# More staging buffers for the first MLP's weights, and its output matrix converted among the second batch's attention steps

## The chip, the cores and the metric

One core of a Trainium2 chip runs the whole program. The metric is the device time of one execution in microseconds; the median of three runs is quoted.

## What is computed

The reference is an attention block with a memory, followed by two MLPs. Cut to what matters:

```python
scores = scale * q @ k.T                     # B=4, H=8, S=576, D=64, causal
local  = softmax(scores) @ v
mem    = phi(q) @ M_prev / (phi(q) @ z_prev)
x = g * mem + (1 - g) * local                # -> 2304 tokens x 512
x = silu(x @ w_in1) @ w_out1                 # 512 -> 2048 -> 512
y = mish(x @ w_in2) @ w_out2                 # 512 -> 2048 -> 512
```

Everything is float32 outside. Inside, each factor of the MLPs' products is split into two float16 parts (a high and a low one), and three matmuls stand for one product.

## The kernel before

The work of a whole program is first recorded as a list of operations, each with a priority, its possible engines and the regions it reads and writes (`Plan.add`). `Plan.issue` (line 97) then goes through a model of the engines: whenever an engine is free it takes, of the operations that are ready, the one with the lowest priority number. The order in which operations are taken is the order in which the instructions stand on each engine, and on the chip each engine goes through them in that order. A priority or a buffer that is changed thus moves instructions everywhere.

**Attention.** There are 32 visits: 16 pairs of heads, first with query tiles 0 and 1 (`VISITS`, line 28), later with tiles 2 to 4. A step is one query tile of one visit: `stage_a` makes scores, exponentials and a DMA transpose of the probabilities (line 559), `stage_b` multiplies with v and the memory, `stage_c` transposes the result (line 610) and writes it to `xd`. Visits 0 to 3 (eight steps) are batch 0; their output is chunk 0 of 256 tokens. `load_kq` and `load_vm` fetch a visit's inputs.

**Weights.** Each MLP's weights are 16 units of 1 MB (`NU`); units 0 to 7 are w_in, 8 to 15 are w_out. `weight_unit` (line 653) loads a unit into a staging buffer `r` and joins its two 32-bit halves to a float32 matrix `w` in slot u + 2 of the array `w_first`: two ScalarE copies, two or three VectorE operations of 1024 columns, and a ScalarE square whose sum gives the maximum `topw`. When eight units are done, `weight_scale` takes the maximum over them (a reduction `mx<-topw` at line 331, a diagonal and a matmul with ones, then the small operations on `cvec`), and `weight_split` writes the high and low parts, one ScalarE copy and one VectorE operation for each unit, in slot u.

The staging buffers of the first MLP's first half are the two `ws` tiles and two pieces of memory that are free early (`g`, `xh`); the second half has the two `ws` alone. A buffer is free again when the unit's square (line 671) has written over it.

**MLP.** A chunk's x is loaded from `xd`, its maximum taken (`chunk_x`), and copied by ScalarE and VectorE to two parts in `xh`. A chunk has eight steps: `gemm1` (24 matmuls, `banks<-xh,w`), `hidden` (tanh from `xsc` on ScalarE, a VectorE operation on `ga` at line 322, and its split into `g`), `gemm2` (24 matmuls, `banks<-g,w`). The first GEMM of layer 0 has two banks, which `hidden` frees. `xsc` holds products of the chunk's scale and of `cvec`, which w_out's maximum completes, so no `hidden` runs before w_out's `weight_scale`. On TensorE the GEMMs have the lowest priority; attention goes first where it is ready.

**Priorities.** The steps of batch 0 have -1.5e5, w_in's units -2e5 and w_out's -1e5 (`W_PRIO`); the steps of the later batches have 2.3 for each step's number, from 18.4 on.

Of the kernel before, what the change touches and what calls it, by code (L numbers as in the profile page):

```python
# [9 lines left out]
F32 = mybir.dt.float32  # L10
F32R = mybir.dt.float32r
U32 = mybir.dt.uint32
# [26 lines left out]
NU = NF  # L39
SPARE = 2  # L40
# [138 lines left out]
def attn_moe_moe2_kernel(ctx: ExitStack, tc: tile.TileContext, kq, vm, beta, w1, w2, out):  # L179
# [22 lines left out]
    def buf(name, shape, dt, n=1):  # L202
        ts = [sb.tile([128, *shape], dt, name=f"{name}_{i}") for i in range(n)]
        return ts

    def ring(tiles):
        state = [0]

        def take():
            state[0] += 1  # L210
            return tiles[(state[0] - 1) % len(tiles)]

        return take
# [14 lines left out]
    w_first, = buf("w", [(NU + SPARE) * 2048], F16)  # L228
# [5 lines left out]

    ws = buf("ws", [1024, 2], U32, 2)
    early = [t[:, 0:4096].bitcast(U32).rearrange("p (n t) -> p n t", t=2) for t in (g_tile, xh)]
    wstages = [ring(ws + early), ring(ws)]
    ga = buf("ga", [2 * TOK], F32, 2)

    spares = [w_first[:, 2048 * NU + 1024 * i:2048 * NU + 1024 * i + 1024].bitcast(F32) for i in range(2 * SPARE)]  # L240
# [55 lines left out]
    def slot(l, u):  # L296
        return (w_first, w_second)[l][:, 2048 * u:2048 * u + 2048]
# [38 lines left out]
    def act(prio, out, in_, func, scale=1.0, bias=0.0):  # L336
        plan.add(prio, [c_act(out, in_, func, scale, bias)], [out], aps(in_, scale, bias) + [tables])

    def ts(prio, out, in0, s1, op0, s2=None, op1=None):
        plan.add(prio, [c_ts(out, in0, s1, op0, s2, op1)], [out], aps(in0, s1), shared=not ps(in0))  # L340

    def stt(prio, out, in0, s, in1, op0, op1):
        plan.add(prio, [c_stt(out, in0, s, in1, op0, op1)], [out], aps(in0, s, in1), shared=not ps(in0) and not ps(in1))

    def tt(prio, out, in0, in1, op, es=("DVE",)):
        plan.add(prio, [(*c_tt(e, out, in0, in1, op), WAIT_R * i) for i, e in enumerate(es)], [out], aps(in0, in1),
                 shared=not ps(in0) and not ps(in1))
# [34 lines left out]
    def dma(prio, out, in_, writes=None, reads=None):  # L382
        nbytes = 128 * cols(out) * SIZE[out.dtype]
        plan.add(
            prio, [("SP", 475, lambda: nc.sync.dma_start(out=out, in_=in_))],
            [out] if writes is None else writes, [in_] if reads is None else reads, tail=nbytes / 360)
# [49 lines left out]
    def load_kq(v, prio):  # L436
        p, _, nk = VISITS[v]
        n = min(S, 128 * nk)
        t = kqr()
        rk[v], rq[v] = t[:, 0, 0:n], t[:, 1]  # L440
        dma(prio, t[:, :, 0:n], kq[p].rearrange("p (t s) -> p t s", t=2)[:, :, 0:n], reads=[])

    def load_vm(v, prio):
        p, _, nk = VISITS[v]
        n = nk * 2 * (D + 1)
        t, rm[v] = rvr()[:, 0:n], rmr()
        rv[v] = t.rearrange("p (n e d) -> p n e d", n=nk, e=2)
        dma(prio, t, vm[p, :, 130:130 + n], reads=[])
        dma(prio, rm[v], vm[p, :, 0:130], reads=[])
# [43 lines left out]
    def prep_phi(v, i0, i1, prio):  # L493

        if v not in er:
            er[v] = er_()
        e, src = er[v][:, 64 * i0:64 * i1], rq[v][:, 64 * i0:64 * i1]
        act(prio, e, src, AF.Exp)
        act(prio, src, src, AF.Relu)
        stt(prio, e, e, 1.0, src, ALU.min, ALU.add)  # L500
# [65 lines left out]
    def stage_b(n, prio):  # L566

        v, qt = STEPS[n]
        R = min(128, S - 128 * qt)
        nk = qt + 1  # L570
        v1, v2, gvv = vv[v]
        vb = bank[6 + qt % 2]
        if qt < 4:
            pw = pts.pop(n).rearrange("p (s e k) q -> p s k e q", s=2, e=2)
        else:
            pw = pts.pop(n).rearrange("p (s k) (e q) -> p s k e q", s=2, e=2)
        ms = []
        for e in range(2):
            o = vb[0:R, 65 * e:65 * e + 65]
            for kb in range(nk):  # L580
                hi, lo = pw[:, 0, kb, e, :], pw[:, 1, kb, e, :]
                ms += [
                    (o, hi, v1[:, kb, e, :], kb == 0, False),
                    (o[:, 0:D], hi, v2[:, kb, e, :], False, False),
                    (o, lo, v1[:, kb, e, :], False, kb == nk - 1)]
        mm(prio, ms + [(vb[0:R, 130:260], er[v][:, 128 * qt:128 * qt + R], rm[v], True, True)])
        if not last(n):
            return
        m = 1 + qt % 2
        g = banks[0:R, 512 * 6:512 * 8].rearrange("p (b c) -> p b c", b=2)[:, 0:m, 0:260].rearrange("p b (a c) -> p b a c", a=4)  # L590
        den, t4, x = denr()[0:R, 0:m], t4r()[0:R, 0:m], xr()[0:R, 0:m]
        each = lambda y: y[0:R].unsqueeze(1).to_broadcast([R, m, 4])
        tt(prio, den, g[:, :, :, D], each(eps), ALU.add)
        other(prio, "DVE", 165, lambda: nc.vector.reciprocal(out=den, in_=den), [den], [den])
        tt(prio, den, den, each(gvv), ALU.mult)
        tt(prio, t4, g[:, :, :, 0:D], den.unsqueeze(3).to_broadcast([R, m, 4, D]), ALU.mult)
        tt(prio, x, t4[:, :, 0:2], t4[:, :, 2:4], ALU.add, ("POOL", "DVE"))
        xts[n] = (x, R)

    def stage_c(n, prio):  # L600

        if not last(n):
            return
        v, qt = STEPS[n]
        p = VISITS[v][0]
        x, R = xts.pop(n)
        m = 1 + qt % 2
        for i in range(m):
            x2, o = x[:, i].rearrange("p e d -> p (e d)"), bank[6 + i][:, 260:260 + R]
            plan.add(prio, [("PE", 56, lambda o=o, x2=x2: nc.tensor.transpose(o, x2, ident[0:R, 0:R]))], [o], [x2, ident],  # L610
                     edge=(107, 56))
        xo = xor_()[:, 0:m * R]
        copy(prio, xo.rearrange("p (b c) -> p b c", b=m),
             banks[:, 512 * 6:512 * 8].rearrange("p (b c) -> p b c", b=2)[:, 0:m, 260:260 + R])
        b, hp = divmod(p, H // 2)
        t0, n = column(b, 256 * (qt // 2)), m * R
        dma(prio, xd[128 * hp:128 * hp + 128, t0:t0 + n], xo, writes=[("xd", hp, hp + 1, t0, t0 + n)])
# [35 lines left out]
    def weight_unit(l, u, prio):  # L653

        r, w = wstages[int(l > 0 or u >= NU // 2)](), slot(l, u + SPARE).bitcast(F32)  # L660
        t = w.bitcast(U32)
        dma(prio, r, W[l][u].bitcast(U32).rearrange("p (n t) -> p n t", t=2), reads=[])
        low, high = r[:, :, 0], r[:, :, 1]
        act(prio, w, high.bitcast(F32), AF.Abs, 2.0**-112)
        ts(prio, t, t, 3, ALU.logical_shift_left)
        stt(prio, t, high, 0x80000000, t, ALU.bitwise_and, ALU.bitwise_or)
        act(prio, low, low, AF.Copy, 2.0**-29)
        tt(prio, t, t, low, ALU.add, ("DVE", "POOL"))
        top = topw[l][:, u:u + 1]

        plan.add(prio, [("ACT", 0.833 * 1024 + 200, lambda: nc.scalar.activation(  # L671
            out=low.bitcast(F32), in_=w, func=AF.Square, accum_out=top))], [top, low], [w, tables])
# [90 lines left out]
    D_B, D_C, D_Q, D_K, D_P, D_V, D_S = 2.5, 3.2, 4.0, 4.0, 3.0, 6.0, 0.5  # L763
    A_RATE, MOE_B, L_V = 2.3, -1e6, 0.0
    att_prio = lambda n, d=0: A_RATE * (n + d) + (ATT_B if n < N0 else 0)
    MOE, W_PRIO, ATT_B = MOE_B, (-2e5, -1e5), -1.5e5

    def prep(v, prio):
        if VISITS[v][1][-1] >= 2:
# [5 lines left out]
    def attention(n0, n1, sbs):  # L775

        for n in range(n0, n1):
            if 0 <= n - LAG - 1 < NS:
                stage_c(n - LAG - 1, att_prio(n - LAG - 1, D_C))
            if 0 <= n - LAG < NS:  # L780
                stage_b(n - LAG, att_prio(n - LAG, D_B))
            if n < NS:
                pr_ = att_prio(n)
                v, qt = STEPS[n]
                qts = VISITS[v][1]
                if qt == qts[0] and v + 1 < len(VISITS):
                    load_kq(v + 1, pr_)
                stage_a(n, sbs, pr_)
                if qt == qts[0]:
                    prep_v(v, att_prio(n, D_B) - D_V)  # L790
                    if v + 1 < len(VISITS):
                        load_vm(v + 1, att_prio(n, L_V))
                if qt == 0 and 2 in qts:
                    prep_q(v, 1, att_prio(n + 2) - D_Q)
                if qt == qts[0]:
                    prep_phi(v, 2 * qts[0], min(2 * qts[-1] + 2, S // 64), att_prio(n, D_B) - D_P)
                if qt == qts[-1] and v + 1 < len(VISITS):
                    prep(v + 1, att_prio(n + 1) - D_K)
# [119 lines left out]
```

## Time and profile before

| | us |
|---|---|
| median of three runs | 1025.33 (1025.13 to 1026.48) |
| the profiled execution's own time | 1025.4 |
| its span | 1023.6 |
| TensorE matmul busy in the span | 948.2 (93%) |
| VectorE busy | 673.4 (66%) |
| ScalarE busy | 642.5 (63%) |
| GpSimd busy | 273.9 (27%) |

The profile has a row for each instruction with its start, its duration, its engine, its line in the code, and what it writes and reads. PE is TensorE's matmul, DVE is VectorE, ACT ScalarE, POOL GpSimd; SPq is the queue of SyncE, which issues nearly all DMAs. A time in brackets is how long the engine stood idle ahead of a row, with what released it. PEclk is the mean granted clock of TensorE as a share of full speed. Consecutive instructions of one engine overlap a little in the rows.

### The profile page before, as it was taken

To read this page: it belongs to the slowest core of one execution; us is meant where nothing else is said; L and a number is where in the kernel's file an instruction comes from. 1 tells how busy PE (TensorE), PEld (TensorE's weight loads), DVE (VectorE), ACT (ScalarE), POOL (GpSimd) and SP (SyncE) were. 2 spreads that over 40 slices of the span, in tenths; PEclk is the share of its full clock that TensorE was granted. 3 is DMA by queue.
4 is the path that set the end of the run, shared out by engine and by line. 5 is a ranking of instruction groups with operands and counts; after the bars stand their busy time and mean duration, and the time that the engine had idled before them with its cause. 6 is when DMAs were issued, how large, how long until landed. Compare 5 with 4: busy or idle time off the path is not lost.

```text
span 1023.6 us, 20794 instructions
## 1 busy us (share of the span) xinstructions
PE 948.2 (93%) x8364; PEld 732.2 (72%) x8364; DVE 673.4 (66%) x1231; ACT 642.5 (63%) x1095; POOL 273.9 (27%) x280
## 2 busy tenths in 40 slices
PE   2436589999999999999999999999999999999998
PEld 1225478888888888888888888766676766766665
DVE  6988687787787878777757756754544545544433
ACT  7977665666666756756667676744555545555544
POOL 1110123343343433432322522212212122222221
PEclk9956589999999999999999999999999999999999
DMA  9767924775787767845353341100100101000000
GB/s 322 230 148 208 228 58 114 162 187 133 183 156 150 151 137 148 176 114 130 105 199 104 104 146 61 42 30 14 42 22 21 32 12 42 22 21 22 1 21 21
DMA packets 149904, 107.93 MB, mean 105 GB/s; under 512 B 111152, under 2 KB 139312, under 8 KB 145712
## 3 DMA queue, kind: packets, MB, share of 16 engines
q1 hardware_dynamic: 149664, 106.60, 40.1%
q8 instruction: 65, 1.06, 0.4%
q14 instruction: 31, 0.25, 0.1%
q10 hardware_dynamic: 144, 0.00, 0.0%
HBM read 66.21 MB, written 14.16 MB: 79 GB/s over the span
## 4 chain that ended last, share of the span: by engine, by line
PE 85%; DMA 6%; DVE 4%; ACT 4%; issue 1%; SPq 0%; POOL 0%; DVEq 0%; POOLq 0%; ACTq 0%
PE banks L375 84%; DMA arena<-arena 2%; DVE w L322 1%; PE banks L610 1%; DMA g<-w 1%; ACT w L314 1%; DMA xs<-xd 1%; ACT arena L314 1%; DMA ws<-w 1%; DVE arena L322 1%; DMA arena<-kq 1%; ACT ws L671 0%; DVE w L328 0%; DVE arena L328 0%; DMA arena<-vm 0%
## 5 line engine op out<-in xcount | busy, mean ns | idle before, releaser
L375 PEld LDWEIGHTS <-w 128*128 128x128 f16 x3456 | 334.8, 98 | 43.3 <-issue 4.2
L375 PEld LDWEIGHTS <-arena 128*128 128x128 f16 (+1 forms) x3168 | 225.5, 101 | 80.1 <-DMA arena<-arena 27.5
L328 POOL TENSOR_TENSOR g<-ga,g 128x512 f16<-128x512 f32 x108 | 144.1, 1335 | 345.7 <-ACT g L314 327.4
L375 PE MATMUL banks<-xh,w 128*128 128x256 f16 x1728 | 213.8, 275 | 2.6 <-DVE ga L322 2.6
L375 PE MATMUL banks<-g,w 128*128 128x256 f16 x1728 | 209.8, 273 | 0.1
L375 PE MATMUL banks<-xh,arena 128*128 128x256 f16 x1728 | 198.6, 273 | 0.0
L375 PE MATMUL banks<-arena,g 128*128 128x512 f16 x864 | 197.4, 379 | 0.0
L375 PE MATMUL banks<-arena 128*128 128x65 f16 (+6 forms) x1728 | 119.0, 235 | 62.1 <-DMA arena<-arena 24.1
L375 PEld LDWEIGHTS <-g 128*128 128x128 f16 x864 | 84.5, 98 | 87.6
L314 ACT ACTIVATE ga<-ga 128x512 f32<-128x512 f32 x108 | 67.6, 628 | 77.5 <-DVE ga L319 53.6
L314 ACT ACTIVATE arena<-arena 128x256 f32<-128x256 f32 (+6 forms) x180 | 101.5, 592 | 18.5 <-PE banks L375 9.5
L322 DVE SCALAR_TENSOR_TENSOR ga<-ga,banks 128x512 f32<-128x512 f32 x108 | 73.7, 683 | 54.2 <-ACT ga L314 53.7
L322 DVE SCALAR_TENSOR_TENSOR arena<-arena 128x256 f16<-128x256 f32 (+6 forms) x144 | 106.1, 746 | 3.9 <-ACT arena L314 3.4
L314 ACT ACTIVATE w<-w 128x512 f32<-128x512 f32 x108 | 66.6, 625 | 47.3 <-DVE w L319 26.3
L314 ACT ACTIVATE arena<-banks,arena 128x128 f32<-128x128 f32 (+4 forms) x144 | 73.9, 545 | 33.9 <-DVE arena L546 25.9
L314 ACT ACTIVATE g<-ga 128x512 f16<-128x512 f32 x106 | 66.3, 626 | 28.7 <-DVE ga L322 28.2
L328 POOL TENSOR_TENSOR arena<-arena 128x256 f32<-128x256 f32 (+1 forms) x48 | 44.0, 916 | 139.1 <-DVE arena L328 89.3
L314 ACT ACTIVATE ga<-banks,xsc 128x512 f32<-128x512 f32 x72 | 49.2, 685 | 49.2 <-PE banks L375 45.5
L546 DVE TENSOR_REDUCE arena<-banks 128x2 f32<-128x256 f32 (+3 forms) x80 | 64.3, 804 | 23.8 <-PE banks L375 19.9
L328 POOL TENSOR_TENSOR g<-w,g 128x512 f16<-128x512 f32 x36 | 41.6, 1156 | 126.2 <-ACT g L314 126.2
L375 PEld LDWEIGHTS banks<-arena 128*128 128x128 f32 (+2 forms) x288 | 42.4, 228 | 32.9 <-ACT arena L314 29.6
L319 DVE TENSOR_SCALAR ga<-banks,xsc 128x512 f32<-128x512 f32 x36 | 27.0, 750 | 51.7 <-PE banks L375 51.6
(95 smaller groups left out, 942.0 us busy)
## 6 DMA issues: line engine op xcount, KB each, us to landing
ws<-w SPq DMA_DIRECT2D x28, 1024.0 KB, 5.3
arena<-kq SPq DMA_DIRECT2D x16, 576.0 KB, 5.0
arena<-vm SPq DMA_DIRECT2D x16, 325.0 KB, 3.4
xs<-xd SPq DMA_DIRECT2D x9, 512.0 KB, 4.6
yd<-w SPq DMA_DIRECT2D x36, 128.0 KB, 1.9
xs<-yd SPq DMA_DIRECT2D x9, 512.0 KB, 3.8
arena<-kq SPq DMA_DIRECT2D x16, 256.0 KB, 3.4
xd<-arena SPq DMA_DIRECT2D x32, 128.0 KB, 2.5
```

What stands on the lines that cost most here:

```text
L314: return ("ACT", ns, lambda: nc.scalar.activation(out=out, in_=in_, func=func, scale=scale, bias=bias))
L319: return ("DVE", ns, lambda: nc.vector.tensor_scalar(out=out, in0=in0, scalar1=s1, scalar2=s2, op0=op0, **kw))
L322: return ("DVE", 1.04 * cols(out) + 160, lambda: nc.vector.scalar_tensor_tensor(out=out, in0=in0, scalar=s, in1=in1, op0=op0, op1=op1))
L328: return (e, ns, lambda: eng.tensor_tensor(out=out, in0=in0, in1=in1, op=op))
L375: nc.tensor.matmul(out=o, lhsT=l, rhs=r, start=a, stop=z)
L546: other(prio, "DVE", 1.04 * cols(both) + 146, lambda: nc.vector.tensor_reduce(out=m1, in_=both, axis=AX, op=ALU.max, negate=True), [m1], [ ...
L610: plan.add(prio, [("PE", 56, lambda o=o, x2=x2: nc.tensor.transpose(o, x2, ident[0:R, 0:R]))], [o], [x2, ident], edge=(107, 56))
```

## The change

The eight units of w_in get eight staging buffers: to `ws`, `g` and `xh` come four pieces of `w_first` itself, slots 10 to 17, which the first half doesn't fill. The eight units of w_out get five: the two `ws`, slots 14 and 15, 16 and 17, and 8 and 9; the last of these and the two `ws` serve again for units 13 to 15. `w_out`'s priority goes from -1e5 to 15, so that its units 8 to 15 stand at 23 to 30, in the range of the second batch's attention steps (18.4 for step 8 to 34.5 for step 15). The loads `load_kq` and `load_vm` get a priority lower by a million, which puts them ahead of the weights' loads.

```diff
-    wstages = [ring(ws + early), ring(ws)]
+
+    room = [w_first[:, 2048 * i:2048 * i + 4096].bitcast(U32).rearrange("p (n t) -> p n t", t=2) for i in range(8, NU + SPARE, 2)]
+    wstages = [ring(ws + early + room[1:] + ws + [room[3], room[4], room[0]] + ws + [room[0]]), ring(ws)]
...
-        r, w = wstages[int(l > 0 or u >= NU // 2)](), slot(l, u + SPARE).bitcast(F32)
+        r, w = wstages[l](), slot(l, u + SPARE).bitcast(F32)
...
-    MOE, W_PRIO, ATT_B = MOE_B, (-2e5, -1e5), -1.5e5
+    MOE, W_PRIO, ATT_B = MOE_B, (-2e5, 15.), -1.5e5
...
-                    load_kq(v + 1, pr_)
+                    load_kq(v + 1, pr_ - 1e6)
...
-                        load_vm(v + 1, att_prio(n, L_V))
+                        load_vm(v + 1, att_prio(n, L_V) - 1e6)
```

The lines behind the first of these stand two further down than in the kernel before: line 559 there is 561 here.

What that makes of the order shows at three places. On SyncE's queue, at the program's start, before (`ws`, `g`, `xh` and `w` as targets are staging buffers, `w` as a source is the weights in HBM; `arena` holds attention's tiles):

```order
L385 DMA arena_98<-vm 128x130
L385 DMA ws_77<-w 128x2048
L385 DMA ws_78<-w 128x2048
L385 DMA g_76<-w 128x2048
L385 DMA xh_75<-w 128x2048
L385 DMA arena_98<-kq 128x2x256
L385 DMA arena_98<-vm 128x260
L385 DMA arena_98<-vm 128x130 x2
L385 DMA arena_98<-kq 128x2x256
L385 DMA arena_98<-vm 128x260
L559 DMA_TRANSPOSE arena_98<-arena_98 128x4x128
```

and after:

```order
L387 DMA arena_98<-vm 128x130
L387 DMA ws_77<-w 128x2048
L387 DMA ws_78<-w 128x2048
L387 DMA g_76<-w 128x2048
L387 DMA xh_75<-w 128x2048
L387 DMA w_73<-w 128x2048 x2
L387 DMA arena_98<-kq 128x2x256
L387 DMA w_73<-w 128x2048 x2
L561 DMA_TRANSPOSE arena_98<-arena_98 128x4x128
```

Eight matrices instead of four stand ahead of the first transpose of attention.

On VectorE, where `xsc` is completed and the first two `hidden` operations follow, before:

```order
L319 TENSOR_SCALAR wsc_0_92<-wsc_0_92 128x1
L328 TENSOR_TENSOR cvec_0_94<-cvec_0_94 128x1
L322 SCALAR_TENSOR_TENSOR arena_98<-arena_98 128x256
L328 TENSOR_TENSOR xsc_89<-cvec_0_94,xsc_89 128x2
L319 TENSOR_SCALAR arena_98<-banks 128x2
L319 TENSOR_SCALAR arena_98<-arena_98 128x2
L546 TENSOR_REDUCE arena_98<-banks 128x2
L322 SCALAR_TENSOR_TENSOR w_73<-w_73,wsc_0_92 128x1024
L322 SCALAR_TENSOR_TENSOR ga_79<-ga_79,banks 128x512
L322 SCALAR_TENSOR_TENSOR ga_80<-ga_80,banks 128x512
```

and after:

```order
L330 TENSOR_TENSOR xsc_89<-cvec_0_94,xsc_89 128x2
L324 SCALAR_TENSOR_TENSOR arena_98<-arena_98 128x256
L330 TENSOR_TENSOR arena_98<-banks,eps_71 128x8
L321 TENSOR_SCALAR arena_98<-banks 128x2
L596 RECIPROCAL arena_98<-arena_98 128x8
L321 TENSOR_SCALAR arena_98<-arena_98 128x2
L330 TENSOR_TENSOR arena_98<-arena_98 128x8
L324 SCALAR_TENSOR_TENSOR ga_79<-ga_79,banks 128x512
L324 SCALAR_TENSOR_TENSOR ga_80<-ga_80,banks 128x512
L321 TENSOR_SCALAR w_73<-w_73,wsc_0_92 128x1024
```

The first split of w_out (`w<-w,wsc`) has moved from ahead of the two `ga` operations to behind them.

On ScalarE, around the copy of chunk 0's x (`xh<-xs,xsc`), after, where `topw<-w` is a unit's square:

```order
L316 ACTIVATE w_73<-w_73 128x1024
L316 ACTIVATE arena_98<-banks,arena_98 128x128
L316 ACTIVATE xh_75<-xs_74,xsc_89 128x1024
L316 ACTIVATE arena_98<-banks,arena_98 128x128
L673 ACTIVATE w_73,topw_0_87<-w_73 128x1024
```

The square there is unit 12's, behind which its buffer (slots 8 and 9, so `w_73` is written) is free for unit 15's load. Before, unit 15 was loaded into a `ws` tile.

## Rows read from the trace of the kernel before

**Rows 1.** Stretches: length, busy us (count) of PE, PEld, DVE, ACT, POOL; PEclk.

```profile
0.00:60.00 60.00, 21.69 (x130) 14.02 (x131) 51.07 (x99) 53.75 (x90) 5.96 (x28) 0.90 0.76 248
60.00:83.64 23.64, 10.85 (x69) 7.01 (x68) 18.62 (x38) 15.62 (x31) 3.78 (x4) 0.50 0.72 172
83.64:118.31 34.67, 22.97 (x147) 16.60 (x147) 29.54 (x65) 25.68 (x50) 3.24 (x6) 0.60 0.83 230
118.31:131.59 13.28, 6.50 (x39) 4.33 (x40) 7.29 (x29) 7.25 (x14) 1.29 (x3) 0.50 0.72 190
131.59:1023.60 892.01, 886.19 (x7979) 690.26 (x7978) 566.89 (x1004) 540.24 (x915) 259.62 (x239) 1.00 0.35 88
```

**Rows 2.** TensorE's waits from 135 us on: total us, times, longest us.

```profile
PE banks L375 <- ACT arena L314: 0.8, 2, 0.6
```

**Rows 3.** Timeline of TensorE: start, us, line, operation, out<-in, count, idle before.

```profile
19.70 1.10 PE L375 MATMUL banks<-arena 128*128 128x65 f16 x8 [12.54 <-DMA arena<-arena]
...
93.38 5.74 PE L375 MATMUL banks<-xh,w 128*128 128x256 f16 x42
...
131.59 6.07 PE L375 MATMUL banks<-xh,w 128*128 128x256 f16 x33 [2.65 <-DVE ga L322]
```

**Rows 4.** Timeline of VectorE, from w_out's maximum to the first `hidden`.

```profile
118.31 0.15 DVE L331 TENSOR_REDUCE mx<-topw 128x1 f32<-128x8 f32 x1
122.61 0.16 DVE L319 TENSOR_SCALAR arena<-banks 128x2 f32<-128x2 f32 x1 [4.15 <-PE banks L375]
...
130.86 1.28 DVE L322 SCALAR_TENSOR_TENSOR ga<-ga,banks 128x512 f32<-128x512 f32 x2
```

**Rows 5.** ScalarE's waits between 60 and 131.6 us.

```profile
ACT w L314 <- DMA ws<-w: 4.6, 4, 2.7
```

**Rows 6.** Issues on SyncE's queue.

```profile
14.11 3.75 SPq L559 DMA_TRANSPOSE arena<-arena  x2
...
102.48 0.34 SPq L385 DMA_DIRECT2D ws<-w  x1
```

**Rows 7.** Timeline of ScalarE: first readings of staged units, and chunk 0's x.

```profile
14.07 1.22 ACT L314 ACTIVATE w<-g 128x1024 f32<-128x1024 f32 x1
...
17.35 1.12 ACT L314 ACTIVATE w<-xh 128x1024 f32<-128x1024 f32 x1
...
89.09 1.14 ACT L314 ACTIVATE xh<-xs,xsc 128x1024 f16<-128x1024 f32 x1
...
109.98 1.14 ACT L314 ACTIVATE w<-ws 128x1024 f32<-128x1024 f32 x1 [0.25 <-DMA ws<-w]
```

**Rows 8.** Groups of VectorE's instructions up to 140 us, each form apart: busy, mean ns.

```profile
L322 DVE SCALAR_TENSOR_TENSOR w<-w,wsc 128x1024 f16<-128x1024 f32 x13 | 17.3, 1357 | 0.0
L322 DVE SCALAR_TENSOR_TENSOR arena<-arena 128x256 f16<-128x256 f32 x19 | 8.5, 455 | 0.0
L328 DVE TENSOR_TENSOR arena<-banks,arena 128x512 f32<-128x512 f32 x8 | 5.5, 689 | 0.1
```

**Rows 9.** Timeline of TensorE behind the gate, at full clock.

```profile
154.21 0.70 PE L375 MATMUL banks<-arena 64*128 64x256 f32 x4
...
154.97 1.47 PE L375 MATMUL banks<-g,w 128*128 128x256 f16 x12
156.28 0.65 PE L375 MATMUL banks<-arena 128*128 128x65 f16 x8
156.77 1.15 PE L375 MATMUL banks<-g,w 128*128 128x256 f16 x9
157.75 0.27 PE L610 MATMUL banks<-ident,arena 128*128 128x128 f32 x1
157.86 0.49 PE L375 MATMUL banks<-g,w 128*128 128x256 f16 x3
```

**Rows 10.** The second maximum of the second MLP's weights: its diagonal on VectorE and TensorE.

```profile
625.47 0.29 DVE L328 TENSOR_TENSOR diag<-ident,mx 128x128 f32<-128x128 f32 x1
...
627.28 0.39 PE L375 MATMUL banks<-diag,onesf 128*128 128x128 f32 x2
```

## The prediction

> **What bounds the kernel now.** I read the stretches first. From 131.59 us to the end TensorE is busy for 886.19 of 892.01 us at a granted clock of 1.00 (2.4 GHz), and the waits of TensorE in that part come to 0.8 us for their largest cause [rows 1, 2]. So behind 131.59 the time is TensorE's own work, and nothing that another engine does there sets the end as long as it stays ahead. In front of it TensorE stands idle for about half of the time, at a clock of 0.50 to 0.60 (that is mostly 1.2 GHz) [rows 1]. The time of the kernel is therefore: the moment at which TensorE's unbroken stretch begins, plus the work that is then still to do. The timeline of TensorE shows that moment: two steps of the first GEMM of chunk 0 run from 93.38 on (42 of their 48 matmuls in one go), then their two banks are full, and the third step starts at 131.59 behind a wait for VectorE's `ga` (line 322), the second operation of `hidden` [rows 3].
>
> What holds `hidden`? The tanh takes its scale from `xsc`, `xsc` takes `cvec`, and `cvec` is finished only by `weight_scale` for w_out, the second half of w1. That begins with the `mx<-topw` reduction at 118.31, when all eight w_out units have been converted [rows 4]. The gate is the conversion of w_out, and the two engines that convert, VectorE and ScalarE, are not full while it waits: VectorE is idle 23.64 - 18.62 = 5.0 us in the stretch to the x of chunk 0, 5.1 in the next and 6.0 in the last, 16.1 us of 71.6 [rows 1]. ScalarE waits 4.6 us for loads of weights in that time [rows 5], and 4.15 us of VectorE's idle time stand right behind the reduction, where it waits for a matmul of attention that is itself queued on TensorE behind a late transpose [rows 4].
>
> **Part by part.** *What is ahead of the gate on VectorE.* In the new order w_out no longer goes ahead of all of the second batch; but four of its eight loads now stand ahead of the first result of attention in SP's order, where it was two, so its conversion can take any free place. Counted in the built order up to the first `ga` operation, VectorE has 228 instructions before and 202 after: all the 16 units' conversions are there in both, and what falls behind the gate is attention of the second batch. The 26: five of 256 wide at 0.46, four of 512 wide at 0.69, one split at 1.36 [rows 8], four score reductions, which are no wider than 512 and which I take at 0.69 too, and twelve small ones (net) at about 0.16, as the small reduction of rows 4. That is 2.3 + 2.8 + 1.4 + 2.8 + 1.9 = 11.2 us of listed time; neighbours on VectorE overlap by up to 0.1 (two of 0.69 take 1.28 in rows 4), and for the 26 I take off 2.2 us: **9.0 us** of real time. If VectorE's idle time stays what it is, the gate moves from 131.6 to **122.6**. If all its idle time behind 60 us went as well, it would be 131.6 - 9.0 - 16.1 = **106.5**. These are my two ends.
>
> *Where between them.* The last w_out unit now decides. Its load goes into the buffer that unit 12 used, so it is issued only when ScalarE has squared unit 12, and in the order that square stands two places behind the copy of chunk 0's x. The copy is at 89.09 [rows 7]; with its 1.14, a small one and a square of about the same length as the copy that is 92. A load took 7.5 us there (issued at 102.48, read at 109.98), and from that reading to the reduction it took 8.3 (109.98 to 118.31) [rows 4, 6, 7]: 107.8. From the reduction to the third step it is 13.3 now; without the 4.15 of the late transpose 9.1. That makes 116.9 without it, and 121.1 with it. I take **117**, since the transpose in question belongs to steps of the second batch of which fewer now stand ahead, and in the new order `hidden` comes ahead of the first split on VectorE.
>
> *What it costs.* The attention that falls behind has to be done by TensorE later, in time that counts. Counted in TensorE's order up to that third step: 18 score matmuls of 128 wide instead of 20, 16 of 256 instead of 20, 126 of 64 and 65 wide instead of 150, 14 memory matmuls instead of 17, 12 transposes instead of 16. In sets: one pair of narrow and two pairs of wide scores, two short and one long product with v, four transposes. At full clock a wide set took 0.76 (154.21 to 154.97), a short product 0.49, a transpose 0.11 [rows 9]; the narrow set I take at no more than the wide one, the long product at 14/8 of the short. Sum: 3 x 0.76 + 2 x 0.49 + 0.86 + 0.44 = **4.6 us**. What VectorE, ScalarE and GpSimd have to do for it is hidden: they are busy for 567, 540 and 260 of the 892 us behind the gate [rows 1]. If that cover were gone, the first to show it would be TensorE's in-order waits for attention.
>
> *Loads moved.* The first transpose of attention now stands behind all eight w_in matrices instead of four. Rows: it was issued at 14.11, and TensorE waited for it until 19.70; the fourth matrix, issued ahead of it, was first read at 17.35 [rows 3, 6, 7]. A matrix takes about 3.3 us (17.35 behind 14.07 [rows 7]), so four more are 13 us. I put this at nothing in the sum, because VectorE and ScalarE have conversions to do in that time and are the fuller engines there, but it is the slower one of the rivals. The Trainium skill (DMA: Bandwidth & Descriptors, section Queues, rings and completion order) says that each DMA engine takes descriptors in ring order, all of SP's from one ring; by that rule the transpose can't overtake the matrices, and the rows above agree; if the delay passes on in full, that is the slower rival below, and if not, the sum stays. The kq and vm loads, given a higher priority, are as many as before, and their buffers still hold them until the older visit is done; I cost them at nothing.
>
> **Sum.** The profiled run took 1025.4 (its span is 1023.6), the median is 1025.33, so I count from the median: 1025.33 - (131.6 - 117) + 4.6 = **1015.3 us**. With the ends: 1025.33 - 25.1 + 4.6 = 1004.8, and 1025.33 - 9.0 + 4.6 = 1020.9.
>
> **Rivals.** *A new gate at the second MLP.* w2's conversion must be done when its first GEMM begins. VectorE had the diagonal of w2's second maximum ready at 625.47 + 0.29, and TensorE took it at 627.28 [rows 10]: 1.5 us of slack. In the new order that matmul stands 156 matmuls ahead of the end of the first MLP instead of 133, 2.5 us earlier in TensorE's stream, and the stream is 10 us earlier; attention, whose memory w2 needs, ends 57 matmuls (6.2 us at 0.109) later in that stream, so some 4 us earlier on the clock. If w2 can't follow any further than that, TensorE waits 10 + 2.5 - 4 - 1.5 = 7 us: 1022; if it can't move at all, 11 us, and the gain is gone: 1026. For it: two buffers pace w2 as before. Against it: VectorE and ScalarE have idle time there too.
>
> *The conversions lose nothing of their idle time, or all of it:* 1020.9 and 1004.8, the ends above.
>
> *Slower: the transposes behind the weights.* If the 13 us of rows 6 and 7 pass on to the whole of batch 0's attention, the x of chunk 0 is copied at 102 instead of 89, the last unit's load is issued 13 us later too, and the gate is at 130: 1025.33 - 1.6 + 4.6 = **1028.3**. It decides from a delay of 10 us on, where the gate's gain equals the 4.6. Against it: in the first 60 us both engines are nearly full (51.07 and 53.75 of 60 [rows 1]), so a delay of 13 at 20 us need not be one at 80. A mild form of the same: the order puts w_out behind steps of the second batch, the gate stays at 131.6 and only the 4.6 us remain: 1029.9.
>
> **Chances.** The forecast (1008 to 1020): 0.62. Nearly no idle time left (1004 to 1008): 0.10. The second gate (1018 to 1026): 0.15. The slower one, with its mild form (1027 to 1031): 0.13. The range 1007 to 1024 holds the forecast's, a part of the next and most of the second gate's. About 0.2% (2 us) is what a measurement of this kernel can tell from no change: faster than 1023.3 is 0.62 + 0.10 + 0.10 of the second gate's; its other 0.05 is within 0.2%, and the 0.13 of the last are slower.
>
> **What would show it.** `mx<-topw` for w_out on VectorE at 106 to 109 instead of 118.31; the third step's matmuls on TensorE at 115 to 119; the copy of chunk 0's x on ScalarE at 88 to 92, as now; the last w_out load issued at about 92; the stretch behind the gate some 4.6 us longer than 892.0, with waits of TensorE of 2 us at most. Wrong: an x of chunk 0 behind 93 (the slower rival); a wait of TensorE for `diag` between 600 and 625 (the second gate); a gate near 122 with VectorE idle as often as now (the sum of work alone).

## The result, and the profile after

The changed kernel took **1012.20 us** (median of four runs, 1011.39 to 1014.18) against 1025.88 for the kernel before in the same comparison: a ratio of 0.987, 95% interval 0.9853 to 0.9887. The forecast was 1015.3, the range 1007 to 1024. The profiled execution took 1011.85; its span is 1009.8.

The stretches of the changed kernel, cut at the same events as [rows 1] (x of chunk 0 loaded, w_out's maximum, the third step); columns as there, the last two being the busy share of the DMA engines and the GB/s they moved:

```profile
0.00:60.00 60.00, 19.76 (x131) 13.55 (x132) 49.83 (x98) 52.88 (x87) 6.40 (x28) 0.91 0.90 275
60.00:85.54 25.54, 11.84 (x73) 7.77 (x72) 20.43 (x41) 18.37 (x37) 3.11 (x4) 0.50 0.74 204
85.54:108.25 22.71, 14.65 (x88) 10.19 (x89) 21.08 (x40) 18.72 (x30) 1.84 (x2) 0.65 0.61 179
108.25:116.28 8.03, 5.99 (x39) 4.22 (x39) 5.72 (x25) 4.74 (x12) 1.15 (x3) 0.50 0.73 214
116.28:1009.80 893.52, 888.86 (x8033) 693.50 (x8032) 561.55 (x1028) 551.97 (x938) 245.62 (x240) 1.00 0.36 90
```

The third step, "the gate" from here on, moved from 131.59 to 116.28, that is 15.3 us; the stretch behind it grew from 892.01 to 893.52, that is 1.5. 15.3 - 1.5 = 13.8 is what the span lost (1023.6 to 1009.8). Most of the gate's gain lies between chunk 0's x and w_out's maximum: 34.67 us before, 22.71 now, with VectorE busy for 21.08 of them. From the maximum to the gate another 5.3 us went (13.28 to 8.03), and ahead of chunk 0's x 1.9 were lost (83.64 to 85.54).

The rows that answer to [rows 3, 4, 6, 7], from the timelines of TensorE, VectorE, ScalarE and SyncE's queue:

```profile
31.97 1.13 PE L377 MATMUL banks<-arena 128*128 128x65 f16 x8
...
116.28 6.24 PE L377 MATMUL banks<-xh,w 128*128 128x256 f16 x33 [0.75 <-DVE ga L324]
```

```profile
85.54 1.22 DVE L333 TENSOR_REDUCE mx<-xs 128x1 f32<-128x1024 f32 x1 [0.30 <-DMA xs<-xd]
...
108.25 0.16 DVE L333 TENSOR_REDUCE mx<-topw 128x1 f32<-128x8 f32 x1 [0.33 <-ACT w L673]
...
115.54 1.28 DVE L324 SCALAR_TENSOR_TENSOR ga<-ga,banks 128x512 f32<-128x512 f32 x2 [0.28 <-ACT ga L316]
```

```profile
92.97 1.13 ACT L316 ACTIVATE xh<-xs,xsc 128x1024 f16<-128x1024 f32 x1
...
100.62 1.17 ACT L316 ACTIVATE w<-w 128x1024 f32<-128x1024 f32 x1 [0.27 <-DMA w<-w]
```

```profile
14.74 1.32 SPq L561 DMA_TRANSPOSE arena<-arena  x1
...
95.50 0.34 SPq L387 DMA_DIRECT2D w<-w  x1
```

TensorE's waits from 116.2 on (total, times, longest): the second is the gate itself, the first one wait at 584.

```profile
PE banks L377 <- POOL g L330: 0.9, 1, 0.9
PE banks L377 <- DVE ga L324: 0.7, 1, 0.7
```

And w2's second maximum on VectorE and its diagonal on TensorE, which answer to [rows 10]; the matmul stands there without an idle time ahead of it:

```profile
609.65 0.16 DVE L333 TENSOR_REDUCE mx<-topw 128x1 f32<-128x8 f32 x1 [0.43 <-ACT ws L673]
```

```profile
611.48 0.39 PE L377 MATMUL banks<-diag,onesf 128*128 128x128 f32 x2
```

### The profile page after: what moved, and what is told of

It is laid out like the page before. It is cut to its first block, busy times and chain, and to the rows that moved or that the text cites. A ratio compares the mean times of both kernels' runs of the same rounds, so it can differ in the third digit from the quotient of the medians.

```text
span 1009.8 us, 20796 instructions
## 1 busy us (share of the span) xinstructions
PE 941.1 (93%) x8364; PEld 729.2 (72%) x8364; DVE 658.6 (65%) x1229; ACT 646.7 (64%) x1100; POOL 258.1 (26%) x277
## 4 chain that ended last, share of the span: by engine, by line
PE 89%; ACT 4%; DMA 3%; DVE 2%; issue 1%; SPq 0%; POOL 0%; ACTq 0%; DVEq 0%; POOLq 0%
PE banks L377 88%; ACT w L316 2%; PE banks L612 1%; DMA ws<-w 1%; DVE w L324 1%; ACT w L673 1%; DMA arena<-arena 1%; DMA xs<-xd 1%; DMA w<-w 1%; ACT arena L316 0%; ACT ws L673 0%; SPq L387 0%; DVE w L330 0%; ACT ws L316 0%; DVE arena L324 0%
## 5 line engine op out<-in xcount | busy, mean ns | idle before, releaser
L330 POOL TENSOR_TENSOR g<-ga,g 128x512 f16<-128x512 f32 x108 | 137.2, 1272 | 352.4 <-ACT g L316 342.0
L377 PE MATMUL banks<-arena 128*128 128x64 f16 (+7 forms) x1728 | 114.4, 232 | 44.3 <-ACT arena L316 29.2
L316 ACT ACTIVATE w<-w 128x512 f32<-128x512 f32 (+2 forms) x124 | 84.8, 693 | 54.9 <-DVE w L321 33.1
L316 ACT ACTIVATE arena<-arena 128x256 f32<-128x256 f32 (+6 forms) x182 | 103.7, 592 | 23.5 <-PE banks L377 14.4
L330 POOL TENSOR_TENSOR arena<-arena 128x256 f32<-128x256 f32 (+1 forms) x47 | 41.2, 876 | 132.0 <-DVE arena L330 96.7
L377 PEld LDWEIGHTS banks<-arena 64*128 64x128 f32 (+2 forms) x288 | 39.9, 222 | 41.0 <-ACT arena L316 36.9
```

The costliest lines, as they stand in the source:

```text
L316: return ("ACT", ns, lambda: nc.scalar.activation(out=out, in_=in_, func=func, scale=scale, bias=bias))
L330: return (e, ns, lambda: eng.tensor_tensor(out=out, in0=in0, in1=in1, op=op))
L377: nc.tensor.matmul(out=o, lhsT=l, rhs=r, start=a, stop=z)
```

## The experiments

Twelve kernels, each beside the kernel before on the same chip (its medians there: 1025.05, 1026.25 and 1025.50 for the three sets). "Gate" is the start of TensorE's third step, "stretch" the rest of the span from there; both are of the profiled execution. Medians of different sets are compared as they stand, though the kernel before itself lies up to 1.2 us apart between the sets.

| kernel | median us | ratio, 95% interval | gate | stretch |
|---|---|---|---|---|
| changed kernel | 1012.20 | 0.987, 0.9853 to 0.9887 | 116.3 | 893.5 |
| buffers alone | 1018.11 | 0.9932, 0.9905 to 0.9959 | 110.9 | 905.9 |
| priority alone | 1024.25 | 0.9992, 0.9979 to 1.0006 | 138.2 | 883.4 |
| loads alone | 1022.98 | 0.9984, 0.9969 to 0.9998 | 127.1 | 895.1 |
| without the loads | 1018.98 | 0.9943, 0.9920 to 0.9965 | 122.7 | 895.0 |
| without the priority | 1016.20 | 0.9904, 0.9883 to 0.9924 | 109.0 | 904.3 |
| w_in in four buffers | 1016.37 | 0.9911, 0.9889 to 0.9932 | 122.7 | 891.9 |
| unit 15 in g | 1010.92 | 0.9853, 0.9834 to 0.9872 | 116.2 | 892.8 |
| early tanh | 1019.79 | 0.9939, 0.9916 to 0.9961 | 103.9 | 914.3 |
| early tanh, w2 in more buffers | 1012.35 | 0.9874, 0.9854 to 0.9894 | 104.6 | 907.3 |
| unit 15 in g, w2 in more buffers | 1010.71 | 0.9861, 0.9840 to 0.9882 | 116.4 | 893.0 |
| unit 15 in g, priority 8 | 1015.58 | 0.9905, 0.9885 to 0.9926 | 107.5 | 908.2 |
| unit 15 in g, priority 22 | 1022.82 | 0.9978, 0.9967 to 0.9989 | 131.7 | 889.4 |

**The three parts apart.** *Buffers alone* takes back the other two (the diff is against the changed kernel):

```diff
-    MOE, W_PRIO, ATT_B = MOE_B, (-2e5, 15.), -1.5e5
+    MOE, W_PRIO, ATT_B = MOE_B, (-2e5, -1e5), -1.5e5
...
-                    load_kq(v + 1, pr_ - 1e6)
+                    load_kq(v + 1, pr_)
...
-                        load_vm(v + 1, att_prio(n, L_V) - 1e6)
+                        load_vm(v + 1, att_prio(n, L_V))
```

> Buffers alone (the staging rings of the changed kernel, the priorities of the kernel before). In the built order VectorE has 175 rows ahead of the first ga operation, where the changed kernel has 197 and the kernel before 223. Theory 'conversion sets the gate, buffers let it run': about 0.35 us for each of 22 rows puts the gate at 108 to 110 (116.3 in the changed kernel), and the attention that falls behind costs TensorE about 3 us: 1007 to 1010. Rival 'the new priority is what pays': near the kernel before, 1022 to 1026. Rival 'the attention loads, which keep their place behind the weights, come late': gate near 109, but waits of TensorE for attention behind it of 3 us and more: 1012 to 1018.

The gate came to 110.9, near the first theory, but the stretch is 12.4 us longer than the changed kernel's, not 3: 1018.11. The third theory's size is missed by 0.1 (1012 to 1018); its reason is looked at below.

```profile
110.90 5.43 PE L377 MATMUL banks<-xh,w 128*128 128x256 f16 x33 [2.80 <-DVE ga L324]
```

*Priority alone* is the new `W_PRIO` on the kernel before:

> w_out's new priority alone, on the kernel before. VectorE has 246 rows ahead of the first ga operation, 23 more than the kernel before. Theory 'conversion sets the gate, buffers let it run': the gate moves some 8 us back, to 138 to 141, TensorE does some 3.5 us of attention ahead of it: 1028 to 1032. Rival 'the new priority is what pays': 1012 to 1018.

Neither came. The gate went back to 138.2, as the first theory said, but the stretch became 8.6 us shorter, not 3.5, and the time is that of the kernel before:

```profile
138.18:1021.60 883.42, 879.21 (x7920) 686.44 (x7919) 560.18 (x970) 541.50 (x910) 252.29 (x238) 1.00 0.34 87
```

TensorE has 59 matmuls fewer behind the gate than in [rows 1] and is busy for 7.0 us less. Counted from each matmul's start to the next one's, the missing attention is 4.6 of the 8.6 us by which the stretch is shorter, about 0.08 for each matmul. Among the rest are 1.2 us of waits for attention that the kernel before has and this one hasn't, and a clock that rose sooner: in the first 10 us behind the gate the granted clock is 0.87 here and 0.76 before (this kernel second).

```profile
131.59:141.59 10.00, 10.00 (x80) 8.04 (x80) 9.79 (x14) 8.55 (x13) 5.07 (x3) 0.76 0.23 58
138.18:148.18 10.00, 10.00 (x80) 7.99 (x80) 9.79 (x15) 9.21 (x16) 5.15 (x3) 0.87 0.04 10
```

Attention that is done while TensorE has nothing else thus pays for a part of a later gate.

*Loads alone* is the earlier kq and vm loads on the kernel before:

> The earlier kq and vm loads alone, on the kernel before. VectorE has 212 rows ahead of the first ga operation, 11 fewer than the kernel before. Theory 'these loads cost and give nothing by themselves': 1022 to 1026, the gate between 127 and 132. Rival 'they take away the short waits of TensorE in attention behind the gate (about 1.4 us of the difference)': those waits gone, and 1 to 2 us less than the first theory's gate alone gives.

1022.98 and a gate of 127.1: the first theory. The short waits for attention did not go (one of 0.96 stands at 197). *Without the loads* is the changed kernel with their old priority:

> The changed kernel with the kq and vm loads at their old priority. VectorE has 206 rows ahead of the first ga operation, 9 more than the changed kernel. Theory 'the loads' priority gives nothing by itself': gate 116 to 120, 1011 to 1016. Rival 'it takes away the short waits behind the gate': 1.5 us and more above the changed kernel even where the gate is the same, with waits of 0.3 to 0.7 us for attention on TensorE.

Both theories fall: the loads' priority is worth 1018.98 - 1012.20 = 6.8 us here, and most of it is in the gate (122.7 against 116.3). SyncE's queue of this kernel shows what changes place: the first two transposes stand behind the loads of the next visits, which stand behind the weights.

```profile
4.50 2.95 SPq L387 DMA_DIRECT2D w<-w  x4
9.39 0.57 SPq L387 DMA_DIRECT2D arena<-kq  x1
11.84 2.79 SPq L387 DMA_DIRECT2D arena<-vm  x2
16.87 0.55 SPq L387 DMA_DIRECT2D arena<-kq  x1
19.27 2.86 SPq L387 DMA_DIRECT2D arena<-vm  x2
24.29 4.01 SPq L561 DMA_TRANSPOSE arena<-arena  x2
```

24.29 instead of 14.74, and TensorE has done 100 matmuls by 60 us instead of 131. Which engine's wait then makes the 6 us was not taken apart further.

**The load of the last unit.** Unit 15 staged in `g`:

```diff
-    wstages = [ring(ws + early + room[1:] + ws + [room[3], room[4], room[0]] + ws + [room[0]]), ring(ws)]
+    wstages = [ring(ws + early + room[1:] + ws + [room[3], room[4], room[0]] + ws + early[:1]), ring(ws)]
```

> The changed kernel with unit 15 staged in g, which is free, and not behind unit 12's square in slots 8 and 9: its load can be issued some 20 us earlier. Theory 'the load chain of the last unit sets the gate' (the prediction's): w_out's maximum 3 to 6 us earlier (102 to 105 where it was 108.25), gate 110 to 113, 1007 to 1010. Rival 'the work of VectorE and ScalarE sets it' (VectorE busy for 21.1 of the 22.7 us ahead of the maximum): maximum within 1.5 us of 108.25, 1010.5 to 1013.5.

The load was issued at 33.27 instead of 95.50, and the maximum did not move:

```profile
33.27 0.38 SPq L387 DMA_DIRECT2D g<-w  x1
```

```profile
108.49 0.16 DVE L333 TENSOR_REDUCE mx<-topw 128x1 f32<-128x8 f32 x1 [0.32 <-ACT g L673]
```

So the load chain did not set the maximum; the work in front of it on VectorE and ScalarE did. Its time is not to be told from the changed kernel's (the intervals overlap).

**Eight buffers for w_in.** w_in staged in the old four, w_out in its five:

> The changed kernel, but w_in staged in the old four buffers (w_out keeps its five). Six instead of eight matrices stand ahead of the first transpose; VectorE has 216 rows ahead of the first ga operation, the changed kernel 197. Theory 'w_in's extra buffers let the conversions run while attention starts': w_in's maximum 4 us later or more, gate 120 to 124, 1015 to 1020. Rival 'eight matrices ahead of the first transpose cost as much as the buffers give': gate 114 to 118, 1009 to 1013.

w_in's maximum came at 51.81 instead of 42.25 and the gate at 122.7: the first theory. Six matrices instead of eight stand ahead of the first transpose there, TensorE's first product is at 25.41 and chunk 0's x at 81.91 instead of 85.54, so the matrices ahead do delay the attention, but the buffers give more than that costs. The later gate isn't the whole account of the 4.2 us, since TensorE has done more attention by then (48 matmuls fewer are left): it also waits ahead of three of the `diag` matmuls that follow (1.2 at 189, 0.5 at 233, 0.8 at 373), where the changed kernel doesn't.

```profile
PE banks L377 <- DVE diag L330: 2.0, 2, 1.2
PE banks L377 <- DVE arena L330: 0.5, 1, 0.5
```

**w_out's priority.** The changed kernel with it back at -1e5:

> The changed kernel with w_out's priority back at -1e5 (buffers and early loads stay). VectorE has 178 rows ahead of the first ga operation, the changed kernel 197. Theory 'the next gate is chunk 1's x, and the new priority is what spares it': the first gate at 108 to 112, but TensorE reaches the end of chunk 0's steps before chunk 1's x is there and waits for its diag by 2 us and more between 150 and 175, with more attention behind the gate: 1013 to 1018. Rival 'with the early loads the new priority is not needed': no such wait, 1006 to 1011.

The gate is 7.3 us earlier and the time 4.0 us longer. The stretch of this kernel:

```profile
108.99:1013.30 904.31, 894.83 (x8076) 697.02 (x8075) 575.61 (x1048) 551.97 (x947) 250.10 (x244) 1.00 0.37 90
```

Against the changed kernel TensorE has 43 more matmuls in it, is busy for 6.0 us more and idle for 4.8 us more (904.31 - 894.83 = 9.48 against 4.66). TensorE's timeline shows where some 2.9 of the idle time stand:

```profile
155.88 0.95 PE L377 MATMUL banks<-arena 64*128 64x256 f32 x4 [0.99 <-ACT arena L316]
...
158.00 0.80 PE L377 MATMUL banks<-diag,onesf 128*128 128x128 f32 x2 [0.95 <-DVE diag L330]
159.19 0.48 PE L612 MATMUL banks<-ident,arena 128*128 128x128 f32 x1 [0.39 <-DVE xsc L333]
...
160.70 0.37 PE L377 MATMUL banks<-g,w 128*128 128x256 f16 x1 [0.57 <-POOL g L330]
...
161.92 1.46 PE L377 MATMUL banks<-arena 128*128 128x65 f16 x14
```

`diag` there is the maximum of **chunk 1's x**; the wait for it alone is 0.95, less than the 2 us that I had expected. TensorE is through with nearly all it has of chunk 0, waits, and its clock falls, to a granted 0.69 over 155 to 166 us: the 14 matmuls at 161.92 took 1.46, the same group 0.83 at full clock. Chunk 1's first step began at 166.2 here. In the changed kernel it began at 163.2, without a wait, 0.1 us behind the end of the operation that makes that x:

```profile
161.79 1.28 DVE L324 SCALAR_TENSOR_TENSOR xh<-xs,xsc,xh 128x1024 f16<-128x1024 f32 x1
```

```profile
163.21 1.47 PE L377 MATMUL banks<-xh,w 128*128 128x256 f16 x12
```

The changed kernel stands at the edge: chunk 0's last matmuls there run to 168.7. A gate that is much earlier meets this one. Buffers alone does the same (waits of 1.1, 0.4 and 0.8 at 160 to 163, chunk 1 from 170.0 on).

Chunk 1's x takes back the lead, and no more than that. By 200 us TensorE has done as many matmuls in this kernel as in the changed one (changed kernel first):

```profile
0.00:200.00 200.00, 135.96 (x1139) 105.38 (x1140) 156.37 (x346) 150.53 (x283) 38.42 (x64) 0.84 0.66 186
0.00:200.00 200.00, 129.61 (x1138) 101.47 (x1139) 156.42 (x342) 149.91 (x282) 37.30 (x64) 0.98 0.67 186
```

The 3.5 us by which its profiled execution is longer are lost behind that. TensorE's waits from 500 to 640 us come to 2.7, against the one of 0.9 in the changed kernel:

```profile
PE banks L377 <- POOL g L330: 1.8, 3, 0.8
PE banks L377 <- DVE diag L330: 0.9, 2, 0.7
```

The second MLP's weights are converted there, and w2's second maximum came at 625.26 instead of 609.65. That they make these waits is tested below for another kernel, for this one it is argued.

Two more values, with unit 15 in `g`: 8 and 22 instead of 15.

> The kernel with unit 15 in g, w_out's priority 8 instead of 15: 180 rows of VectorE ahead of the first ga operation instead of 198. Theory 'the gate and chunk 1's x have to be balanced, and 15 is near the balance': gate at 110 to 113, stretch behind it 5 us or more above 893, 1012 to 1016. Rival 'an earlier gate pays as long as the attention still comes first in places': 1006 to 1010.

> The kernel with unit 15 in g, w_out's priority 22: 229 rows of VectorE ahead of the first ga operation instead of 198. Theory 'balance': the gate at 125 to 129, the stretch behind it 4 to 8 us shorter (more attention done ahead), 1012 to 1017. Rival 'attention done in the idle time is free, as the stretch of 883 with the priority alone hints': 1005 to 1010.

```profile
107.49:1015.70 908.21, 897.71 (x8076) 699.35 (x8075) 575.30 (x1043) 556.57 (x952) 248.44 (x246) 0.99 0.36 90
```

```profile
131.65:1021.10 889.45, 884.02 (x7964) 689.73 (x7963) 568.19 (x996) 540.78 (x915) 253.23 (x240) 1.00 0.35 88
```

Priority 8 is 4.7 us slower than 15: earlier gate, longer stretch, the wait for chunk 1's `diag` again (at 157.5), and one of 2.0 at 611, ahead of the second MLP. Priority 22 is 11.9 slower, more than I expected: its gate is 15.5 us later and its stretch only 3.4 shorter. 15 is near the balance, and the slope is steeper on the side of the late gate.

**The gate itself.** `xsc` completed by two operations, so that the tanh doesn't wait for w_out:

```diff
-        tt(prio, sc[:, 1:3], cvec[l][:, 1:3], p.to_broadcast([128, 2]), ALU.mult)
+        for i in (1, 2):
+            tt(prio, sc[:, i:i + 1], cvec[l][:, i:i + 1], p, ALU.mult)
```

> The changed kernel with xsc completed by two operations: the tanh's scale takes w_in's part of cvec alone, and only the scale of the output waits for w_out's maximum. In the order eight hidden steps stand ahead of w_out's first split. Theory 'the gate is that dependency, and TensorE is idle ahead of it': up to six steps of the first GEMM (144 matmuls at 0.109, 15.7 us at full clock) go ahead, the second GEMM starts at 118 to 124: 1000 to 1007. Rival 'VectorE and ScalarE set the end of the conversions, and what TensorE gains it gives back at chunk 1's x': a wait for diag between 130 and 170, 1009 to 1015.

The dependency is real: the third step follows the first two directly, at 103.9 (in the 36 matmuls of this row), and from 96.86 to 123.9 TensorE has no idle time.

```profile
103.24 4.09 PE L377 MATMUL banks<-xh,w 128*128 128x256 f16 x36
```

But the time, 1019.79, is above what either theory gave. By 587.0 us TensorE had done 3,072 matmuls of the first MLP, the changed kernel by 586.5. The lead was gone long before, by 200 us (594 matmuls of the first MLP against 597), in waits at 125 to 128 and, for chunk 1's x, at 159 to 165. The rest was lost at the second MLP: w2's second maximum came at 628.78 instead of 609.65, and TensorE waited. Its waits from 600 to 640 us:

```profile
PE banks L377 <- DVE diag L330: 1.9, 1, 1.9
PE banks L377 <- DVE xh L324: 1.2, 1, 1.2
PE banks L377 <- POOL g L330: 1.1, 1, 1.1
PE banks L377 <- ACT g L316: 1.0, 1, 1.0
```

The changed kernel has none there. Attention ended at 505.1 instead of 495.6, and w2 takes its memory. The test of that place is the same kernel with w2 staged like w1:

```diff
...
+    room2 = [w_second[:, 2048 * i:2048 * i + 4096].bitcast(U32).rearrange("p (n t) -> p n t", t=2) for i in range(8, NU + SPARE, 2)]
+    wstages[1] = ring(ws + room2[1:] + ws + ws + [room2[3], room2[4], room2[0]] + ws + [room2[0]])
```

> The early tanh again, and w2 staged as the change stages w1 (six and five buffers, of w2's own place), so that its conversion is not paced by two buffers. Theory 'what the early tanh wins it gives back at the start of the second MLP, where w2's second maximum came at 628.8 (609.6 in the changed kernel) and TensorE waited 5.6 us and lost 1.7 by its clock': that maximum at 610 to 620, these waits gone, 1011 to 1015. Rival 'VectorE and ScalarE pace w2, not its buffers': maximum within 4 us of 628.8, 1017 to 1021.

```profile
611.82 0.16 DVE L335 TENSOR_REDUCE mx<-topw 128x1 f32<-128x8 f32 x1 [0.44 <-ACT arena L675]
```

The maximum is 17 us earlier, the waits from 600 on are gone, and the time fell by 7.4 us to 1012.35. Put on the kernel with unit 15 in `g`, where TensorE doesn't wait for w2, the same buffers give nothing that can be measured, though w2's second maximum moves to 590.9:

> The kernel with unit 15 in g, and w2 staged in the added buffers. There TensorE waits 0.9 us in all between the gate and the end, so theory 'the second MLP's start is no gate in the changed kernel': 1009.5 to 1012, as with unit 15 in g alone, though w2's second maximum comes earlier. Rival 'w2's conversion takes places on VectorE that TensorE feels all over the last 100 us before the second MLP': 1005 to 1009.

None of the variants beats the changed kernel by more than the intervals allow; the two with unit 15 in `g` are the lowest.

## Why the prediction was right, and where not

**The bound** held: TensorE's unbroken stretch begins at the gate, and 15.3 us of gate gave 13.8 of span.

**The gate** was put at 117 and came at 116.3. Its steps: the x copy at 89 came at 92.97, just outside the 88 to 92; the last load at 92 came at 95.50; from there to the reading 5.1 us instead of 7.5, and from the reading to the maximum 7.6 instead of 8.3. The sum, 108.25, is within 0.5 of the forecast, since the late start and the shorter load offset each other. But the reason is **wrong**: with unit 15 in `g` that load is 62 us earlier and the maximum stays (108.49), so that the sum came out was luck. What sets it is the work ahead: VectorE is busy for 21.08 of the last 22.71 us, and over the three kernels with unit 15 in `g` the maximum follows the rows that stand ahead of it on VectorE: 161 rows 99.94 (priority 8), 177 rows 108.49 (15), 205 rows 120.85 (priority 22), 0.44 to 0.53 us for each row. ScalarE's rows go with them (137, 152, 173), so the runs don't show which of the two engines sets it. The two terms of the ends can be read from the windows: up to the gate VectorE was busy for 106.5 us before and 97.1 after, 9.5 less where I had counted 9.0; and of its idle time 5.9 us went (7.1 less behind 60 us, 1.2 more ahead of it), where the ends had 0 and 16.1. So the count of work was right, and the share of the idle time was the guess that came out. From the maximum to the gate it took 8.0 against 9.1; the 4.15 for a late transpose [rows 4] went, as I took it.

**The cost behind the gate**, 4.6 us, was the term of the sum that was mis-sized: the stretch grew by 1.5, and that is the 3.1 us by which the forecast was too high. (The gate's other 0.7 us doesn't show: the spans lie 13.8 apart, the medians 13.1 from the 1025.33 that I counted from.) The counts were right: 24 more narrow products, 12 more records of scores (a matmul in float32 has two), 6 of the memory, four transposes, 54 attention records in all with six masks and two sums. From each matmul's start to the next one's the attention took 3.7 us more, not 4.6 (scores with their masks 1.8 instead of 2.3, products with v and the memory 1.4 instead of 1.8, transposes 0.2 instead of 0.4, and 0.3 that I had not counted). And the same matmuls of the first MLP took 1.6 less, the part from the second MLP's first matmul on 0.6 less (386.70 to 386.08): 3.7 - 1.6 - 0.6 = 1.5. The listed waits don't make the 1.6: the kernel before waits 0.6 at 200 and 0.4 at 440, for attention, the changed kernel 0.9 at 584. The rest are delays of a few tenths of a us or less. No one part of the change can be named for the waits: priority alone has none, loads alone and the kernel without the loads have one at 197 (1.0 and 1.6). What decides them stays open.

**"The loads I cost at nothing"** gave the right sum, since the gate was read from an order that held them, but as an account of the parts it is wrong: with buffers and priority they are worth 6.8 us, alone 2.

**The rivals.** The transposes behind eight matrices did come late: the first was issued at 14.74 and landed at 30.86, 0.5 us behind the eighth matrix; in the kernel before it landed at 19.65 (landing times of the trace). TensorE's first product is at 31.97, 12.3 us later than in [rows 3], close to the 13 us of that rival. (The 3.3 us for a matrix were a wrong reading: the matrices landed 2.5 us apart in both kernels, 3.3 is the distance of ScalarE's first readings of two.) The Trainium skill (DMA: Bandwidth & Descriptors, section Queues, rings and completion order) has it that a DMA engine takes descriptors in ring order, and these times agree. But the delay didn't pass on: chunk 0's x came 1.9 us later (85.54 against 83.64), while VectorE and ScalarE had conversions to do (busy for 49.83 and 52.88 of the first 60 us), as the argument against that rival had it. The second gate, w2, did not close in the changed kernel: w2's second maximum came 15.6 us earlier, as much as the gate. It is real all the same: the early tanh ran into it. The rival that I did not have is **chunk 1's x**: it is what met the earlier gate in buffers alone, without the priority, with priority 8 and with the early tanh. It took their lead; what they lose beyond that comes later (for buffers alone in part), and their waits behind 200 us stand nearly all from 500 us on. The trace of the kernel before could have raised the question, what TensorE does when chunk 0's eight steps (some 50 us) are through: that x is there at 142.66, far ahead of the end of these steps, and in the new order the steps end sooner.

```profile
142.66 1.22 DVE L331 TENSOR_REDUCE mx<-xs 128x1 f32<-128x1024 f32 x1 [0.48 <-DMA xs<-xd]
```

The low end, 1004.8, supposed that a gate at 106.5 costs only 4.6. At 107.5 to 110.9 the stretch was 904 to 908, so that end was not to be had in this way.

## What to carry to other kernels

When the busiest engine waits for a gate, look for the next gate before counting the gain: list when each later input of that engine will be ready, and the gain ends at the first that it catches up with. Work of that engine that can be done in its idle time has a price too, here about 0.07 us for each attention matmul (54 took 3.7 us, 59 took 4.6), so the best place of a conversion is a balance that has to be measured on both sides. Parts of one change that look like nothing alone (the early loads: 2 us; the priority: 0.8, within the noise) can be what makes the main part pay.

## What the runs showed that I had not expected

The clock of a stretch can be missing at the start of a profile. The trace's list of granted clocks begins at 99.9 us for the early tanh (at 44.2 in the kernel before), and what lies ahead of its first entry is printed as full clock. For the early tanh the stretch from 60 to 110 us prints a granted clock of 1.00:

```profile
60.00:110.00 50.00, 32.18 (x217) 22.90 (x216) 42.01 (x84) 37.74 (x69) 8.17 (x8) 1.00 0.70 191
```

but three matmuls of the same shape took 0.88 at 94.94 and 0.49 at 109.18:

```profile
94.94 0.88 PE L377 MATMUL banks<-xh,w 128*128 128x256 f16 x3
...
109.18 0.49 PE L377 MATMUL banks<-xh,w 128*128 128x256 f16 x3
```

The first took what such three take at 1.2 GHz (0.85 at 95.75 in the changed kernel, in a stretch of 0.50 to 0.65). The 0.90 and 0.91 of the first 60 us, in [rows 1] and in the stretches above, are too high for the same reason: the eight matmuls at 19.70 [rows 3] took 1.10, eight such 0.65 at full clock [rows 9]. Where the printed clock and the durations of equal matmuls differ, I went by the durations.
